# Starting the first feed-forward group on half of its tokens, packed apart, in a fused linear-attention and maxout kernel

## The chip, the cores and the metric

One NeuronCore of a Trainium2 chip runs the whole program. The metric is the device time of one execution in microseconds (us). Times are medians of several runs; a ratio is the mean time of one kernel's fast runs over the mean of the other's fast runs of the same rounds, so it is not quite the ratio of the medians quoted. The span of a profile is 1.7 to 1.9 us (once 2.0) shorter than the time of the same run.

## The reference

```python
# q, k, v, f_logit: (4 batches, 8 heads, 768 tokens, 48); fp32
f = 1 / (1 + exp(-f_logit))
for t in range(768):                       # per batch and head
    state = f[t][:, None] * state + outer(k[t], v[t])
    y[t] = q[t] @ state
x = y.transpose(0, 2, 1, 3).reshape(3072, 384)
h = maximum(maximum(x @ w1, x @ w2), x @ w3)        # 384 x 768 each
out = h @ w_out                                     # 768 x 384
```

The kernel cuts the sequence into 24 units of 128 tokens (64 of each of two batches). Four units make a group of 512 tokens, the width of one feed-forward (FFN) matmul.

## The kernel before

Each unit's attention part is split into stages that the program interleaves by hand: `sigmoids`, `after` (scan of the gates from behind, then kh), `before` (scan from the front, then qh), `keys` (transposes), `pairs`, `values`, `finish`. The FFN of a group is a generator, and `fill(n)` runs n of its steps between attention stages of the next group, so that TensorE never stands.

```python
def round_begin(n):      # ScalarE, two passes over raw piece n
def round_middle(n):     # VectorE max and shift (L224, L225), GpSimd add (L227)
def round_end(n):        # VectorE merge into w_in or w_out (L234)

def pack(u0, u1, xT, queues=one):      # heads -> xT: TEN DMAs, whatever the number of tokens
    ...
def ffn(g, xT):
    for j in range(NJ):                # 6 column blocks
        for i in range(3):             # w1, w2, w3: one "step", 512 tokens wide
            ... 3 matmuls into p
            if i == 0: nc.scalar.copy(top, p)
            else:      nc.vector.tensor_tensor(hm[:, j, :] if i == 2 else top, p, top, op=ALU.max)
            if g == 0: ... round one piece, begin another, load_weights(2, r + 1)
            yield
    ... 4 output blocks (w_out), a yield behind each

def busy(n): ...                       # n dummy matmuls, 256 wide

# ... (loads and units 0 to 2)
load_weights(3); load(GRP, one, "fk")  # f and k of unit 4
pairs(3); busy(1); round_begin(2); round_middle(2)
values(3); round_end(0)
finish(3)                              # state update L359, heads of unit 3
round_end(1); round_end(2)
pack(0, GRP - 1, xT, both)             # all 512 tokens, SyncE and ScalarE
for n in range(3, 5): round_begin(n); round_middle(n)
busy(14)                               # dummies while xT is packed
load(GRP, one, "q"); load_v(GRP); load_weights(3); load(GRP + 1); load_v(GRP + 1)
pending.append(ffn(0, xT))
fill(1); sigmoids(GRP); after(GRP); fill(1); before(GRP); carry(GRP); fill(1)
# ... units 4 to 23, four fills each
fill(8)
# tail: least = min(ends); one matmul over it (L581); fill(99)
```

## Time and profile before

| | before |
|---|---|
| median (range) beside the changed kernel | 488.15 us (487.48 to 489.26, 4 runs) |
| span of the profiled run | 487.8 us (a further run, of 489.5 us) |
| TensorE busy | 466.6 us, 96% |
| end of unit 3's state update, T | 33.3 us |
| first FFN matmul | 42.1 us |
| pairs of unit 8 (start) | 112.15 us |

From unit 8 on both kernels do nearly the same work in nearly the same order, so the start of the pairs of unit 8 is a good milestone. The lines of the profile are in the prediction.

### The profile page before, as it was taken

The numbers are of one execution on the slowest core, as the hardware profiler recorded it, in microseconds if no ns is written. First come the engines' busy times: TensorE is split into PE (matmuls) and PEld (weight loads), VectorE is DVE, ScalarE is ACT, GpSimd is POOL, SyncE is SP. The second block draws the span as 40 slices with busy tenths as digits, with TensorE's granted clock in tenths as the row PEclk, the third lists the DMA queues.
The fourth block names the chain that finished last, engine by engine and source line by source line (L and its number), as shares of the span: only waits on it lengthen the run. The fifth ranks groups of instructions, "written<-read, shape, count | busy, mean of one in ns | idle before, by whom it ended". The sixth has DMA issues, their size and how long they took to land.

```text
span 487.8 us, 10037 instructions
## 1 busy us (share of the span) xinstructions
PE 466.6 (96%) x4101; PEld 252.5 (52%) x4101; DVE 223.2 (46%) x346; ACT 109.4 (22%) x227; POOL 99.5 (20%) x132
## 2 busy tenths in 40 slices
PE   5779999998999999999999999999999999989994
PEld 4666465555454446555546554556554445434452
DVE  7954999993263462263462253462354320112110
ACT  2344445333022112122112122122121112000000
POOL 2122456553120220211220211220211300000000
PEclk9979999999999999999999999999999999999998
DMA  9987999633664042565042674033630012100012
GB/s 128 161 201 202 257 233 198 92 76 66 110 87 66 1 79 47 101 83 84 1 79 53 106 91 66 0 67 65 107 43 1 1 48 50 32 1 1 0 23 48
DMA packets 170008, 38.51 MB, mean 79 GB/s; under 512 B 154977, under 2 KB 168801, under 8 KB 169953
## 3 DMA queue, kind: packets, MB, share of 16 engines
q1 hardware_dynamic: 166208, 36.50, 42.6%
q10 hardware_dynamic: 3744, 1.28, 1.3%
q8 instruction: 34, 0.56, 0.5%
q14 instruction: 22, 0.17, 0.1%
HBM read 28.31 MB, written 4.72 MB: 68 GB/s over the span
## 4 chain that ended last, share of the span: by engine, by line
PE 87%; SPq 5%; DMA 3%; DVE 1%; ACT 1%; issue 1%; POOL 0%; ACTq 0%; DVEq 0%; POOLq 0%
PE p L401 55%; PE p L422 19%; SPq L159 3%; PE y L342 3%; PE y L372 2%; PE a L328 2%; PE y L351 2%; PE p L448 2%; PE tr L315 1%; SPq L174 1%; DMA raw<-in_moe_w_dram 1%; PE tr L243 1%; DMA k_ld<-in_k_dram 1%; SPq L389 1%; DMA v_ld<-in_v_dram 1%
## 5 line engine op out<-in xcount | busy, mean ns | idle before, releaser
L401 PE MATMUL p<-xT,w_in 128*128 128x512 f32 x648 | 288.1, 596 | 0.7 <-ACT top L405 0.7
L401 PEld LDWEIGHTS p<-xT,w_in 128*128 128x128 f32 x648 | 120.0, 190 | 138.4 <-issue 132.0
L422 PE MATMUL p<-w_out,hm 128*128 128x384 f32 x288 | 96.6, 490 | 0.5 <-DVE w_out L234 0.5
L407 DVE TENSOR_TENSOR top<-p,top 128x512 f32<-128x512 f32 x36 | 24.7, 687 | 119.1 <-PE p L401 118.9
L422 PEld LDWEIGHTS p<-w_out,hm 128*128 128x128 f32 x288 | 53.8, 190 | 38.1 <-issue 2.4
L405 ACT COPY top<-p 128x512 f32<-128x512 f32 x36 | 21.1, 586 | 179.2 <-PE p L401 179.2
L407 DVE TENSOR_TENSOR hm<-p,top 128x512 f32<-128x512 f32 x36 | 24.8, 690 | 50.5 <-PE p L401 50.5
L288 POOL COPY ends<-r 128x8 f32<-128x8 f32 x24 | 4.7, 194 | 189.3 <-DVE r L282 189.3
L227 POOL TENSOR_TENSOR top_bits<-top_bits,rest_bits 128x384 uint32<-128x384 uint32 x24 | 28.3, 1178 | 40.2 <-DVE top_bits L225 25.5
L427 ACT COPY o<-p 128x384 f32<-128x384 f32 x24 | 11.5, 477 | 106.8 <-PE p L422 103.6
L296 DVE TENSOR_TENSOR_SCAN prod<-gate,from_inv 128x520 f32<-128x520 f32 x24 | 34.7, 1448 | 0.0
L282 DVE TENSOR_TENSOR_SCAN r<-gate,from_one 128x520 f32<-128x520 f32 x24 | 30.9, 1289 | 2.8 <-issue 2.1
L378 ACT COPY heads<-y 64x256 f32<-64x256 f32 (+1 forms) x72 | 26.6, 369 | 9.5 <-PE y L372 8.3
L331 DVE TENSOR_TENSOR at<-a,mask 128x512 f32<-128x512 f32 x24 | 16.5, 688 | 24.9 <-PE a L328 24.9
L300 POOL TENSOR_TENSOR qh<-qt,prod 128x512 f32<-128x512 f32 x16 | 18.8, 1178 | 38.1 <-DVE qt L247 38.1
L342 PEld LDWEIGHTS y<-at,v_ld 64*64 64x64 f32 x768 | 14.4, 137 | 18.1 <-issue 15.0
L289 POOL TENSOR_TENSOR kh<-kt,r 128x512 f32<-128x512 f32 x16 | 19.7, 1233 | 14.0 <-DVE kt L247 14.0
L317 ACT COPY ks<-tr 128x512 f32<-128x512 f32 x22 | 12.9, 585 | 39.3 <-PE tr L315 39.0
L306 POOL TENSOR_TENSOR state<-st,ends 128x384 f32<-128x384 f32 x22 | 20.4, 925 | 0.2
L342 PE MATMUL y<-at,v_ld 64*64 64x64 f32 x768 | 18.0, 228 | 2.5 <-ACT heads L378 1.4
L247 DVE STREAM_TRANSPOSE gate<-sig 128x512 f32<-128x512 f32 x16 | 11.3, 708 | 16.8 <-ACT sig L263 16.8
L224 DVE TENSOR_SCALAR top_bits<-top_bits 128x384 f32<-128x384 f32 x24 | 12.6, 525 | 9.9 <-ACT top_bits L212 9.9
(66 smaller groups left out, 286.5 us busy)
## 6 DMA issues: line engine op xcount, KB each, us to landing
raw<-in_moe_w_dram SPq DMA_DIRECT2D x18, 384.0 KB, 6.0
v_ld<-in_v_dram SPq DMA_DIRECT2D x48, 96.0 KB, 3.1
out_dram<-o SPq DMA_DIRECT2D x48, 96.0 KB, 2.2
raw<-in_moe_w_out_dram SPq DMA_DIRECT2D x6, 384.0 KB, 5.8
xT<-heads SPq DMA_DIRECT2D x30, 72.0 KB, 2.2
f_ld<-in_f_logit_dram SPq DMA_DIRECT2D x32, 64.0 KB, 2.6
k_ld<-in_k_dram SPq DMA_DIRECT2D x32, 64.0 KB, 2.6
q_ld<-in_q_dram SPq DMA_DIRECT2D x32, 64.0 KB, 2.5
```

Source lines behind the costliest of these rows:

```text
L227: nc.gpsimd.tensor_tensor(top, top, rest, op=ALU.add)
L282: nc.vector.tensor_tensor_scan(r[:, 0:LEN][:, ::-1], flat(gate)[:, ::-1], flat(from_one)[:, ::-1], 1.0, op0=ALU.mult, op1=ALU.max)
L289: (nc.vector if u < BY_ROWS else nc.gpsimd).tensor_tensor(kh.rearrange("p h a t -> p a h t"), kt, by_batch(r[:, 1:LEN + 1].rearrange("p (x ...
L296: nc.vector.tensor_tensor_scan(flat(prod), flat(gate_tiles[u % 2]), flat(from_inv[u % 2]), 1.0, op0=ALU.mult, op1=ALU.max)
L300: (nc.vector if u < BY_ROWS else nc.gpsimd).tensor_tensor(qh, qt, by_batch(prod[:, :, 1:]), op=ALU.mult)
L306: nc.gpsimd.tensor_tensor(t, states[u % 2], ends[:, u, :].unsqueeze(2).to_broadcast([128, 2 * HP, D]), op=ALU.mult)
L342: nc.tensor.matmul(y[o:o + DP, a, hp * C:(hp + 1) * C], lhsT=v_ld[s, 2 * hp + par, :], rhs=d["at"][s, par, hp, :], start=(hp == 0), stop=F ...
L378: nc.scalar.copy(heads[o, :, t0 + a * C:t0 + (a + 1) * C], y[i, a, 0:HP * C].rearrange("p (h t) -> p h t", h=HP))
L401: nc.tensor.matmul(p, lhsT=w_in[i][:, kt, j * 128:(j + 1) * 128], rhs=xT[:, kt, :], start=(kt == 0), stop=(kt == NK - 1))
L405: nc.scalar.copy(top, p)
L407: nc.vector.tensor_tensor(hm[:, j, :] if i == 2 else top, p, top, op=ALU.max)
L422: nc.tensor.matmul(p[:, 0:DM], lhsT=hm[:, j, i * UT:(i + 1) * UT], rhs=w_out[:, j, :], start=(j == 0), stop=(j == NJ - 1))
```

## The change

The intent: TensorE passes some 8 us before the first FFN matmul with dummies. Pack the first 256 tokens (units 0 and 1) as soon as they are there, begin the group on them in half-wide steps, and do the other half when units 2 and 3 are packed. To make room, rounding moves behind the first units, and loads go out from two queues. Not in the cut diff: the scan is split from `after`, the stages of units 0 to 3 are reordered, the first two state copies go from VectorE to ScalarE, and xT of the first group is laid out by halves. The core of the diff, with cuts and with comments of mine:

```diff
-                load_v(0)
-                load(2)
-                load(3, one, "f")
-                load_v(1)
...
+                load_v(0, act)                 # ScalarE's queue
+                load(2, act, "k")
+                load_weights(3)                # weights ahead of f of unit 3 and v of unit 1
+                load(3, one, "f")
...
+                load_v(1, act)
...
+                pack(0, 1, xT, one, 0)         # ten DMAs more
+                load_weights(3)
+                load(GRP, one, "fk")
...
-                pack(0, GRP - 1, xT, both)
-                busy(14)
+                pack(2, 3, xT, (nc.sync, nc.scalar, nc.sync, nc.scalar, nc.sync), 1)
+                round_begin(3)
...
+            J_HALF = 2
+                steps = [(j, slice(0, TOK)) for j in range(NJ)]
+                if g == 0:    # 12 half steps, then 12 full ones
+                    steps = [(j, slice(n * HALF, (n + 1) * HALF)) for n in range(2) for j in range(J_HALF)] + steps[J_HALF:]
...
+                            ahead = n_step + 2 if n_step <= 6 else 8 + (2 * n_step - 11) // 3 if n_step <= 12 else n_step
...
-                    fill(1)
+                    fill(1 if u < 2 * GRP else 2)        # a full step now takes two fills
...
-                fill(8)
+                fill(12)
                 least = ...
+                fill(6)                                  # three steps behind the reduction
```

## The prediction

> **What bounds the kernel now.** I read the page first, then TensorE's waits after the first feed-forward (FFN) matmul, then busy time by stretch, then the timeline around the start of the FFN. Busy time of the page, and TensorE's waits from 42 us on:
>
> ```profile
> PE 466.6 (96%) x4101; PEld 252.5 (52%) x4101; DVE 223.2 (46%) x346; ACT 109.4 (22%) x227; POOL 99.5 (20%) x132
> ...
> PE a L328 <- POOL qh L300: 1.4, 1, 1.4
> PE tr L581 <- DVE least L579: 1.3, 1, 1.3
> PE p L401 <- ACT top L405: 0.7, 1, 0.7
> PE p L422 <- DVE w_out L234: 0.5, 1, 0.5
> ```
>
> Once the FFN has begun, TensorE waits 1.4 + 1.3 + 0.7 + 0.5 = 3.9 us in all. So the span is 42.1 (start of the first FFN matmul) + 435.3 (work) + 3.9 (waits) + 6.5 (last output copy and stores, 481.3 to 487.8) = 487.8. Only the start and the waits can change.
>
> Busy time by stretch; columns: us from:to, length, then busy us and count of PE, PEld, DVE, ACT, POOL, then granted clock, DMA share, GB/s:
>
> ```profile
> 10.00:12.00 2.00, 2.00 (x43) 1.61 (x41) 1.97 (x4) 0.89 (x2) 0.19 (x1) 1.00 1.53 151
> 31.00:32.00 1.00, 1.00 (x51) 1.00 (x44) 0.72 (x2) 0.42 (x1) 0.10 (x1) 0.50 0.93 207
> 33.30:42.10 8.80, 8.74 (x61) 7.43 (x62) 3.76 (x9) 3.02 (x7) 1.31 (x2) 0.76 0.53 113
> 42.10:45.90 3.80, 3.80 (x16) 2.13 (x15) 0.23 (x1) 1.05 (x3) 1.09 (x1) 1.00 0.77 164
> 45.90:108.50 62.60, 62.05 (x647) 33.70 (x646) 59.96 (x102) 28.34 (x60) 35.50 (x39) 1.00 0.88 181
> ```
>
> Until 33 us run the attention parts of units 0 to 3. From 45.9 to 108.5 both TensorE (99%) and VectorE (60.0 of 62.6, 96%) are full: VectorE rounds 24 weight pieces beside the first FFN group. Between 33.3 and 45.9 VectorE works only 4.0 us of 12.6. The timeline says why; columns: start, us, engine, line, operation, [idle before <- releaser]:
>
> ```profile
> 32.75 0.56 DVE L359 TENSOR_TENSOR st<-y,state 128x384 f32<-128x384 f32 x1 [0.99 <-PE y L351]
> 34.39 7.84 PE L448 MATMUL p<-from_one,ident 128*128 128x256 f32 x28
> 35.70 3.19 ACTq L389 DMA_DIRECT2D xT<-heads  x5
> 39.53 0.36 DVE L224 TENSOR_SCALAR top_bits<-top_bits 128x384 f32<-128x384 f32 x1 [4.82 <-ACT top_bits L212]
> 42.08 2.74 PE L401 MATMUL p<-xT,w_in 128*128 128x512 f32 x6
> 45.92 0.36 DVE L224 TENSOR_SCALAR top_bits<-top_bits 128x384 f32<-128x384 f32 x1 [3.58 <-ACT top_bits L212]
> ```
>
> TensorE fills 34.4 to 42.2 with dummy matmuls (L448) while xT is packed by DMA. VectorE waits 4.8 us for ScalarE, which is issuing five packing DMAs, and then 3.6 us for ScalarE again, which waits for the first full 512-wide FFN product.
>
> **What the Trainium skill says.** (1) "TensorE: Matmul & The Clock Gate", Part 1: an idle TensorE drops to half clock and needs a busy window of some 3.4 us to come back. The trace agrees: granted 0.50 in 31:32, still 0.76 on average in 33.3:42.1. (2) The same page, "Back-to-back issue gap": the gap grows linearly with columns, plus 2.5 ns. Six 512-wide records take 2.58 us in the chain (430 ns each), so a 256-wide one costs an estimated 215 ns: halves cost TensorE nothing. (3) "DMA: Bandwidth & Descriptors", "Issuing engines are not separate DMA queues": a second issuing engine saves only issue time. Here too: from 10 to 12 us one queue alone gives DMA share 1.53 at 151 GB/s, so the 192-byte rows already saturate it, and the second queue can only reorder. (4) "SBUF — State Buffer", "Who interferes with whom": some VectorE forms and GpSimd block each other on a shared port. L224 takes 0.35 us alone and up to 1.16 us beside GpSimd, so VectorE's queue from 45.9 to 108.5 cannot be shrunk by moving work about.
>
> **The change, part by part.** I write T for the end of the state update of unit 3 (L359): 32.75 + 0.56 = 33.3 before.
>
> *T itself.* Rounding leaves ScalarE's and VectorE's queues ahead of unit 3, and two state copies (0.56 us each) leave VectorE. That is worth about 3 us (1.4 us of TensorE behind ScalarE's copies, two roundings at about 1.1 us). Against it: ScalarE must issue four loads (v of unit 0, k of unit 2) before the sigmoid of unit 1. Each reuses one of eight DMA semaphores and waits until the load eight places earlier has landed; at 98 KB and 150 GB/s (0.655 us each) I count the fourth issued near 11.8, so that sigmoid ends at 12.4 instead of 10.3. Also three weight loads (1.2 MB, some 4 us) now precede f of unit 3, whose scan comes 1 to 1.5 us late. Walking VectorE's order with the trace's durations (scans 1.2, products 0.6 to 0.7) gives T = 32.5, a gain of only 0.8.
>
> *Start.* With the fourteen dummies gone and half A of xT packed long before, the first FFN matmul begins at T + 0.9 = 33.4 rather than 42.1: 8.7 us earlier.
>
> *What is given back at once.* The first six half steps (6 x 215 ns = 1.29 us each) need pieces 0 to 5, rounded just ahead. After T VectorE does pieces 1 and 2 in part (1.7 us), then waits for ScalarE's first pass over piece 3, which stands behind three copies of heads (1.14) and four packing DMAs (4 x 0.62 = 2.5): until about T + 5.2. Then one piece (1.1 alone, 1.4 beside GpSimd) plus a 256-wide max (0.35) per step paces TensorE: step 3 starts at T + 6.4, step 4 at 7.9, step 5 at 9.4, step 6 at 10.7 and ends at T + 12.0. Unhindered they would end at T + 0.9 + 7.7 = 8.6. So 3.4 us go back, and another 1 us around step 10, which waits for the max behind unit 4's scan. The half clock of the first two steps hides in the same wait.
>
> *The rest of the group.* VectorE's work from T to the last w_out rounding was 63.9 us (8.8 + 3.8 + 62.6 minus idle of 5.0 + 3.6 + 2.6), and 66.2 to the transposed q of unit 8 at 110.8. Now it is 66.2 + 0.65 (piece 2) + 0.24 (split maxes) = 67.1. Its idle shrinks from 11.3 to an estimated 6 (3.5 for piece 3, 1 for late raw pieces 9 to 11, 1.5 in small ones). So q of unit 8 comes at T + 73.1, and after GpSimd (1.3) the pairs of unit 8 start at T + 74.4. TensorE's own account is T + 0.9 + 68.1 (work from 42.1 to 112.15 less 2.0 waits) + 4.4 = T + 73.4. They nearly meet: VectorE decides by 1 us. With T = 32.5 that point moves from 112.15 to 106.9: 5.2 us earlier, not 8.7.
>
> *Tail.* The minimum over ends is now issued three units before the matmul that needs it, so the 1.3 us wait at L581 goes. From unit 8 on TensorE's order is unchanged.
>
> Sum: 5.2 + 1.3 = 6.5 us, 487.9 - 6.5 = 481.4; I record 481.3.
>
> **The rivals.** *A: nothing paces it.* If rounding kept up with the half steps, the whole 8.7 + 1.3 us plus most of the later waits (2.6) would come: 475 to 478. For it: the pieces are scheduled two steps ahead. Against: a half step lasts 1.29 us and a piece with its max 1.5 to 1.75 us, and VectorE is 96% full already. *B: the loads eat it.* If ScalarE's blocked loads and the weights ahead of unit 3 cost 3 us more than I count, T is 35 to 36 and the time 484 to 485. For it: DMA is saturated from 4 to 18 us. Against: the same bytes arrive before unit 3's v in both kernels. *C: the SyncE queue.* Packing now takes 16 issues on it rather than 5, and raw pieces 9 to 23 queue behind them; ScalarE would stall on raw tiles and the group end 2 to 3 us later: 483.5. The 12 pieces fetched ahead speak against.
>
> **Range and chances.** T is uncertain by 1.5 us, VectorE's idle by 2, the start by less; together about 3 us either side, with rival A's side a little longer: 477.3 to 484.8. Faster by over 2% means below 478.1, which needs rival A nearly whole: 0.14. Slower by over 2% needs a lost order of loads far beyond B: 0.01. Within 2%: 0.85.
>
> **What would show it.** Right: first FFN matmul near 33 to 34; a VectorE wait of 3 to 4 us for top_bits after the packing DMAs on ScalarE; TensorE waits of 4 to 6 us on w_in and on maxes between 33 and 60; pairs of unit 8 near 107; no wait for "least". Wrong: T under 31 or over 34.5; TensorE waiting little in the half steps (A); long waits for raw or f in the first 30 us (B) or for raw after 45 (C).

## The result, and the profile after

The changed kernel took **496.69 us** (496.54 to 496.98, 4 runs) against 488.15 us: ratio 1.0173, 95% interval 1.0153 to 1.0194. I had predicted 6.5 us less; it is 8.5 us more. The profiled run has a span of 494.8 us. (The two profiles differ by 7.0 us and not by 8.5, as that of before is of a run 1.4 us above the median.)

TensorE's waits from 30 us on in the changed kernel; columns: engine, tile, line waiting <- what it waited for: us in total, times, longest.

```profile
PE p L426 <- DVE w_in L235: 3.3, 2, 2.2
PE a L333 <- POOL qh L305: 1.9, 1, 1.9
PE p L426 <- DVE hm L433: 1.5, 1, 1.5
...
PE p L426 <- DMA xT<-heads: 0.8, 1, 0.8
PE p L426 <- DVE top L433: 0.7, 1, 0.7
```

The wait for "least" is gone, as predicted. In its place stand waits for rounded weights, for maxima, for xT and for qh. TensorE's timeline of the same stretch (start, us, engine, line, operation, count of records, [idle before <- releaser]) shows where; a half or full step is six records, `busy(n)` 2n:

```profile
36.88 1.13 PE L426 MATMUL p<-xT,w_in 128*128 128x256 f32 x4
38.84 1.97 PE L426 MATMUL p<-xT,w_in 128*128 128x256 f32 x8 [0.83 <-DMA xT<-heads]
42.98 1.78 PE L426 MATMUL p<-xT,w_in 128*128 128x256 f32 x6 [2.17 <-DVE w_in L235]
45.92 6.62 PE L426 MATMUL p<-xT,w_in 128*128 128x256 f32 x18 [1.17 <-DVE w_in L235]
...
58.60 1.56 PE L426 MATMUL p<-xT,w_in 128*128 128x256 f32 x6 [0.73 <-DVE top L433]
61.63 2.86 PE L426 MATMUL p<-xT,w_in 128*128 128x256 f32 x12 [1.47 <-DVE hm L433]
...
66.22 1.98 PE L426 MATMUL p<-xT,w_in 128*128 128x512 f32 x4
```

The first FFN matmul begins at 36.9 us, 5.2 us earlier than before. But the twelve half steps (72 records, some 15.9 us at the 0.221 us that a record takes in e10 below, and 2.9 us of unit 4's and 5's transposes and pairs among them, 18.8 in all) last until 66.2, that is 29.3 us: **10.5 us are lost inside them.** 6.4 of these are the five waits shown. About 3 are slow clock: 18 records take 6.62 us where 4.0 would do. The rest is small gaps.

SyncE's own timeline shows its queue, which issues in order; first the kernel before:

```profile
35.31 4.77 SPq L389 DMA_DIRECT2D xT<-heads  x5
40.18 1.34 SPq L159 DMA_DIRECT2D q_ld<-in_q_dram  x2
...
51.25 4.57 SPq L200 DMA_DIRECT2D raw<-in_moe_w_dram  x6
```

and the changed kernel:

```profile
28.60 7.13 SPq L399 DMA_DIRECT2D xT<-heads  x10
...
44.47 3.73 SPq L399 DMA_DIRECT2D xT<-heads  x6
48.25 1.65 SPq L201 DMA_DIRECT2D raw<-in_moe_w_dram  x3
49.99 1.37 SPq L160 DMA_DIRECT2D q_ld<-in_q_dram  x2
...
60.59 3.14 SPq L201 DMA_DIRECT2D raw<-in_moe_w_dram  x6
```

Packing by halves takes twenty DMAs instead of ten, since a DMA moves one head's piece whatever its number of tokens, and 16 of them are now on SyncE, about 0.6 to 0.7 us each. So everything behind the packing comes late: SyncE's part of the second packing, itself behind f and k of unit 4, begins at 44.5 us, q of unit 4 is issued at 50.0 instead of 40.2, and raw piece 12 at 60.6 us.

Later, at unit 8 (TensorE's timeline of the changed kernel):

```profile
118.85 0.88 PE L333 MATMUL a<-qh,kh 48*64 48x64 f32 x32 [1.94 <-POOL qh L305]
119.66 7.53 PE L452 MATMUL p<-w_out,hm 128*128 128x384 f32 x18
```

The pairs of unit 8 come at 118.85 instead of 112.15, 6.7 us later. Behind that wait the granted clock falls (0.80 from 118 to 120, 0.50 from 120 to 122 us), which costs another 1.45 us: 24 records of L452 last 9.39 us, before 7.94. So the profile adds up: -5.2 (earlier start) + 7.3 (more waiting up to unit 8) + 4.6 (slow clock and small gaps up to there) + 1.45 - 1.3 (tail) = +6.9, against +7.0 measured.

### The profile page after: what moved, and what is told of

The parts are those of the page before. It is cut to its first block, busy times and chain, and to the rows that moved or that the text cites. A ratio compares the mean times of both kernels' runs of the same rounds, so it can differ in the third digit from the quotient of the medians.

```text
span 494.8 us, 10088 instructions
## 1 busy us (share of the span) xinstructions
PE 466.6 (94%) x4111; PEld 256.9 (52%) x4111; DVE 219.8 (44%) x348; ACT 110.1 (22%) x231; POOL 101.1 (20%) x132
## 4 chain that ended last, share of the span: by engine, by line
PE 85%; DMA 5%; DVE 4%; SPq 1%; ACT 1%; issue 1%; ACTq 1%; POOL 0%; DVEq 0%; POOLq 0%
PE p L426 55%; PE p L452 19%; PE y L347 3%; PE y L377 2%; PE a L333 2%; PE y L356 2%; DMA v_ld<-in_v_dram 2%; PE tr L320 1%; DMA q_ld<-in_q_dram 1%; DMA f_ld<-in_f_logit_dram 1%; PE tr L244 1%; SPq L399 1%; DVE prod L301 1%; DMA raw<-in_moe_w_dram 1%; DVE w_in L235 1%
## 5 line engine op out<-in xcount | busy, mean ns | idle before, releaser
L426 PE MATMUL p<-xT,w_in 128*128 128x512 f32 (+1 forms) x684 | 292.4, 580 | 7.1 <-DVE w_in L235 3.3
L426 PEld LDWEIGHTS p<-xT,w_in 128*128 128x128 f32 x684 | 128.1, 192 | 142.3 <-issue 126.5
L452 PE MATMUL p<-w_out,hm 128*128 128x384 f32 x288 | 97.7, 495 | 0.0
L433 DVE TENSOR_TENSOR top<-p,top 128x512 f32<-128x512 f32 (+1 forms) x38 | 25.0, 659 | 122.3 <-PE p L426 122.1
L452 PEld LDWEIGHTS p<-w_out,hm 128*128 128x128 f32 x288 | 54.7, 193 | 38.4 <-issue 4.1
L431 ACT COPY top<-p 128x512 f32<-128x512 f32 (+1 forms) x38 | 21.4, 563 | 181.6 <-PE p L426 181.6
L433 DVE TENSOR_TENSOR hm<-p,top 128x512 f32<-128x512 f32 (+1 forms) x38 | 25.1, 662 | 52.1 <-PE p L426 52.0
L228 POOL TENSOR_TENSOR top_bits<-top_bits,rest_bits 128x384 uint32<-128x384 uint32 x24 | 28.1, 1170 | 37.7 <-DVE top_bits L226 29.3
L301 DVE TENSOR_TENSOR_SCAN prod<-gate,from_inv 128x520 f32<-128x520 f32 x24 | 35.2, 1466 | 0.0
L283 DVE TENSOR_TENSOR_SCAN r<-gate,from_one 128x520 f32<-128x520 f32 x24 | 29.7, 1239 | 6.2 <-ACT gate L261 3.3
L305 POOL TENSOR_TENSOR qh<-qt,prod 128x512 f32<-128x512 f32 x16 | 18.8, 1176 | 38.9 <-DVE qt L248 38.9
L347 PEld LDWEIGHTS y<-at,v_ld 64*64 64x64 f32 x768 | 13.6, 134 | 18.8 <-issue 15.1
L294 POOL TENSOR_TENSOR kh<-kt,r 128x512 f32<-128x512 f32 x16 | 19.7, 1234 | 13.7 <-DVE kt L248 13.0
L347 PE MATMUL y<-at,v_ld 64*64 64x64 f32 x768 | 17.0, 224 | 3.3 <-DMA v_ld<-in_v_dram 1.9
L333 PE MATMUL a<-qh,kh 48*64 48x64 f32 x768 | 16.4, 225 | 2.3 <-POOL qh L305 1.9
```

The lines of the kernel that those rows point to most:

```text
L228: nc.gpsimd.tensor_tensor(top, top, rest, op=ALU.add)
L283: nc.vector.tensor_tensor_scan(r[:, 0:LEN][:, ::-1], flat(gate)[:, ::-1], flat(from_one)[:, ::-1], 1.0, op0=ALU.mult, op1=ALU.max)
L294: (nc.vector if u < BY_ROWS else nc.gpsimd).tensor_tensor(kh.rearrange("p h a t -> p a h t"), kt, by_batch(r[:, 1:LEN + 1].rearrange("p (x ...
L301: nc.vector.tensor_tensor_scan(flat(prod), flat(gate_tiles[u % 2]), flat(from_inv[u % 2]), 1.0, op0=ALU.mult, op1=ALU.max)
L333: nc.tensor.matmul(p[t, par, hp * C:(hp + 1) * C], lhsT=kh[r, hp, a, :], rhs=qh[r, a, hp, :], start=True, stop=True)
L347: nc.tensor.matmul(y[o:o + DP, a, hp * C:(hp + 1) * C], lhsT=v_ld[s, 2 * hp + par, :], rhs=d["at"][s, par, hp, :], start=(hp == 0), stop=F ...
```

## The experiments

Eighteen kernels ran, in five batches on five chips. Each batch has its own runs of the kernel before, and there they scatter more: 486.1 to 492.5 us. That scatter goes with the granted clock of the run: in one batch 486.07 us at 0.999, 489.37 at 0.990, 490.66 at 0.985. So I read shares of 1 us or less from the traces, not from the medians. "Pairs of unit 8" is the milestone named above; ratios are against the kernel before.

| run | what | median us | ratio (95%) | T | pairs of unit 8 |
|---|---|---|---|---|---|
| e1 | after, loads of before | 495.88 | 1.014 (1.007, 1.021) | 33.6 | 117.7 |
| e2 | before, loads of after | 492.00 | 1.008 (1.001, 1.015) | 37.4 | 114.3 |
| e3 | after, piece 3 begun early | 497.03 | 1.019 (1.011, 1.026) | 35.0 | 117.5 |
| e4 | after, dummies in the waits | 497.89 | 1.019 (1.012, 1.026) | 35.9 | 119.9 |
| e5 | after, e1 + e3 + queue reordered | 495.41 | 1.016 (1.012, 1.021) | 32.7 | 116.4 |
| e6 | after, cheap rounding (wrong) | 494.44 | 1.015 (1.010, 1.019) | 36.1 | 116.2 |
| e7 | before, cheap rounding (wrong) | 487.72 | 1.001 (0.997, 1.005) | 32.0 | 108.5 |
| e8 | before, three half steps | 491.79 | 1.010 (1.005, 1.015) | 31.9 | 113.4 |
| e9 | e5, cheap rounding (wrong) | 494.86 | 1.011 (1.005, 1.016) | 35.1 | 119.9 |
| e10 | e9 with 12 dummies | 495.31 | 1.013 (1.008, 1.018) | 34.3 | 117.9 |
| e11 | before, late fill and tail moved | 486.98 | 0.995 (0.991, 0.999) | 32.6 | |
| e12 | after, late fills put back | 501.20 | 1.027 (1.022, 1.032) | 35.2 | |
| e13 | after, no loads of units 4, 5 (wrong) | 497.20 | 1.019 (1.014, 1.024) | 37.3 | 119.4 |
| e14 | e13, cheap rounding (wrong) | 487.57 | 0.997 (0.993, 1.002) | 36.7 | 110.5 |
| e15 | e14, loads of before (wrong) | 488.43 | 0.999 (0.995, 1.004) | 33.8 | 111.5 |
| e16 | after, half steps undone | 495.27 | 1.012 (1.006, 1.017) | 40.2 | 119.5 |
| e17 | e8, loads moved | 490.90 | 1.004 (1.001, 1.006) | 32.7 | 113.2 |
| e18 | e11, dummies ahead of v of unit 3 | **483.86** | 0.989 (0.987, 0.992) | 31.5 | |

(Pairs of unit 8 are left out where a block was moved across them.) T of the seven profiles that have the changed kernel's loads and half steps (the changed kernel, e3, e4, e6, e12 to e14) lies from 35.0 to 37.3, mean 36.1; of the five with half steps and the loads of before (e1, e5, e9, e10, e15) from 32.7 to 35.1, mean 33.9. So the loads move T by some 2 us, and one profile by itself can be as far off.

### First: which single part does it? (e1 to e4)

**e1** puts the order of loads of before into the changed kernel, **e2** the order of after into the kernel before:

```diff
 e1: +load_v(0); load(2); load(3, one, "f"); load_v(1); load(3, one, "kq"); load_v(2); load_weights(3); load_v(3); load_weights(3)
     -load_v(0, act); load(2, act, "k"); load_weights(3); ... load_v(1, act) ...
 e2: the reverse, in the kernel before
```

> The changed kernel with the load order and queues of the kernel before (all on SyncE's queue, the first weights behind v of unit 2); everything else of the change stays. Theory L (the new loads make the attention part late: end of unit 3's state update at 36.2 instead of 33.3): that point comes back to 32.5 to 33.5, the first FFN matmul to 33.5 to 34.5, and the time falls by about 3 us to 493.5. Rival D (VectorE's total work up to the last rounded piece decides, as I predicted): it also falls by about 3. Rival Q (raw pieces and queue decide): the time stays within 1 us of 496.7.

> The kernel before with the load order and queues of the changed one, nothing else. Theory L: end of unit 3's state update moves from 33.3 to about 36, the first FFN matmul from 42.1 to 45, the time rises by about 3 us to 491. If the loads are harmless by themselves and only the interplay hurts: 488, within 1 us.

e1 brought T back to 33.6 us, and the time hardly moved: 495.88. In place of the late start its TensorE waits 2.4 us for xT, 2.5 for q of unit 4 and 1.4 for top. e2 came out at 492.0 with T = 37.4, so the loads by themselves do harm in a kernel without half steps (though the interval of its ratio begins at 1.0005). Where the time goes is in the chain of the changed kernel (start, us, what):

```profile
14.46 8.48 DMA v_ld<-in_v_dram
22.93 0.04 issue
22.98 0.62 PE y L347 x25
```

v of unit 1, issued by ScalarE at 13.8 and 14.5 us, lands only at 22.9. In the kernel before it was issued at 14.1 and 14.8 us, no earlier, and TensorE had it at 19.7. New ahead of it are three weight loads of 384 KB, issued at 12.4 to 13.9; a second queue did not get it past them. That these three are the reason is read from the order: no run moved them alone. f of unit 3, issued at 15.2 and 15.9, took 7.8 us to land as well, and in e2 the chain runs through f and not through v:

```profile
16.10 7.94 DMA f_ld<-in_f_logit_dram
```

There TensorE waits 2.1 us for f of unit 3 and nothing for v.

**e3** begins piece 3 ahead of ScalarE's packing DMAs, **e4** puts 5 and 3 dummies into the two waits before half steps 3 and 4:

```diff
 e3:  round_begin(2)
     +round_begin(3)                     # was behind pack(2, 3, ...)
 e4: +warm = {2: 5, 3: 3}.get(n_step, 0) if g == 0 else 0
     +for _ in range(warm): nc.tensor.matmul(pw, lhsT=ident, rhs=from_one..., start=True, stop=True)
```

> The changed kernel with ScalarE's first pass over weight piece 3 moved ahead of its four packing DMAs; one call moved. Theory R (the half steps wait for rounded pieces because the first pass stands behind those DMAs): the VectorE wait of 3.8 us at 37.8 goes, half step 3 starts near 41 instead of 43.0, step 4 near 43 instead of 45.9, and the time falls by 2 to 3 us; by 5 to 6 if the closed gaps also keep the clock up (theory C on top). Rival D (VectorE's total decides): the wait only moves, the time stays within 1 us of 496.7.

> The changed kernel with five dummy matmuls in TensorE's wait before half step 3 and three before step 4, about as long as the waits (2.2 and 1.2 us). Theory C (the waits drop the granted clock to 0.50 from 44.4 to 50.9, and steps 4 to 6 take 6.6 us instead of 3.9): the clock stays at 1.00, the time falls by 2.5 to 3 us. If VectorE paces the steps anyway (theory R alone): steps 4 to 6 end no sooner, the time stays within 0.7 us of 496.7.

Neither gained. In e3 the wait for w_in shrank from 3.3 to 0.8 us, and q of unit 4 was then 2.6 us late. In e4 the clock stayed at 1.00 through the half steps, and what it saved turned into a wait of 2.9 us for q and 1.7 for top. So the slow clock, 3 of the 10.5 us lost, was no cause: it hid behind a supply that came later anyway.

### Then: which supply? (e5 to e7, e9, e10)

**e5** is e1 and e3 with SyncE's queue reordered (all loads of unit 4 right behind the packing, pieces 12 and 13 ahead of unit 5). **e6** and **e7** cut the rounding of each piece to its last VectorE operation, in the changed kernel and in the one before:

```diff
 e5: +load(GRP)                          # f, k, q right behind pack(2, 3, ...)
     +load_weights(2, 2); pending.append(ffn(0, xT)); fill(2); load(GRP + 1); load_v(GRP + 1); fill(4)
 e6, e7: round_begin, round_middle: -all
         round_end: -by(top)  +by(hi)
```

> The changed kernel with the loads of before (as e1), piece 3 begun early (as e3), and SyncE's queue reordered behind the packing: f, k and q of unit 4 directly behind the second packing, weight pieces 12 and 13 ahead of unit 5's loads, and those two half steps later. Theory S (after the packing the in-order queue delivers q of unit 4 and pieces from 12 on too late; in e1 and e3 TensorE waited 2.5 us for q and VectorE 3.5 us for piece 12 at 60 to 64): both waits shrink to under 1 us, and the time falls by 3 to 5 us to 492 or 493. If VectorE's and GpSimd's rounding itself is the pace in that stretch (theory R): the waits go but the time stays within 1.5 us of e1 (495.9).

> The changed kernel with the rounding of each weight piece cut to one VectorE operation (wrong values on purpose: no ScalarE passes, no GpSimd addition, one VectorE operation instead of three). Theory R (rounded pieces pace the half steps): with no rounding to wait for, the waits on w_in and maxes go, the clock stays up, the first FFN matmul comes at 34 to 36 and the time falls by 10 us or more, to 483 to 486, below the cheap kernel of before. Theory S (loads and queue): waits for q of unit 4 and for raw pieces take their place, the time stays above 490.

> The same cut of the rounding in the kernel before. It never waited for rounded pieces except 0.5 us, and its start is set by the packing: both theories expect only what ScalarE's freed queue gives at the start, 1 to 2 us, so 486 to 487.

e5 (495.41) no longer waits more than 0.7 us for a load of unit 4, but 2.4 us for top, 1.5 for hm, 2.1 for xT. e6 (494.44) has no wait for rounding, but one line stands out in TensorE's timeline:

```profile
55.53 1.09 PE L229 MATMUL tr<-ident,q_ld 128*128 128x128 f32 x4 [4.62 <-DMA q_ld<-in_q_dram]
```

q of unit 4, again issued at 49.3 us, landed 5.3 us later behind three raw pieces. I had expected e6 to tell whether rounding was the bound; it told that rounding is not the only one. e7 shows that rounding doesn't bound the kernel before: 487.72, its ratio 1.001.

**e9** joins e5 and e6, **e10** adds `busy(12)` before the first half step:

> The reordered queue of e5 together with the one-operation rounding of e6 (wrong values on purpose). Each alone left the time at 494 to 495; in e5 the TensorE waits were the rounding's (top 2.4, hm 1.5 us), in e6 the load's (q of unit 4, 4.6 us). Theory S+R (two supplies, the rounding and the queue of loads, bound the early stage side by side, so that removing one uncovers the other): the waits for top, hm and q of unit 4 all vanish, full steps begin by about 60 us instead of 63.9 to 64.2, and the time falls by some 3.9 to 4.6 us to about 491. Rival L (the stage near 112 to 119 us, with the chain to qh of unit 8, is a fixed date): full steps begin earlier but the pairs of unit 8 stay near 116 us and the time stays 494 to 495.

> e9 with 12 dummy matmuls ahead of the first half step, so that it begins with all of xT there and at full clock. In e5 the first 36 matmuls lasted from 33.7 to 46.9 us: three waits for xT of 2.1 us in sum and half the clock from 36 to 42 us. Theory S+R with a third term, cold start (the clock): dummies end at about 36.1, the 36 matmuls take 36 x 0.22 = 7.9 us and end at 44.0, some 2.9 us earlier than in e9, and the time falls by as much, to about 488. If the clock hides behind other waits, as in e4, the time is that of e9 within 1 us.

Both missed: 494.86 and 495.31. The waits for top, hm and q went as expected, and pairs of unit 4 came at 60.0 and 59.1 us; but then TensorE waited 4.0 and 3.9 us for f of *unit 5*, which my order had put behind raw pieces 12 and 13. I had moved the shortage, not removed it. To take it away the loads themselves had to go.

### The deciding pair (e13, e14), and e15

**e13** is the changed kernel without the 16 loads of units 4 and 5; their tiles keep the tokens of units 0 and 1. Its output is wrong, which doesn't matter for the time. **e14** adds the cheap rounding of e6. **e15** adds to that the loads of before and piece 3 begun early.

```diff
 def load_tokens(dst, src, u, queues=one):
+    if u in (GRP, GRP + 1):
+        return
```

> The changed kernel without the 16 loads of units 4 and 5 (f, k, q and v; the tiles keep the tokens of units 0 and 1, wrong values on purpose). SyncE, which issues in order and spent 0.65 to 0.85 us on each DMA between 28 and 60 us, gets some 10 us back. Theory Q (SyncE's issuing, made longer by ten more packing DMAs, is what ate the gain): the raw piece 12, issued at 60.6 us, comes by about 50, the wait for hm at 61.6 and those for q of unit 4 cannot arise, full steps begin 2 to 4 us earlier than 66.2, time 493 to 494.5. Theory R (the rounding, alone, once the loads are no bound): time as of the changed kernel within 1 us.

> The same with the one-operation rounding (wrong twice on purpose). In e6, with the cheap rounding alone, the only large wait was 4.6 us for q of unit 4. Theory Q+R (two supplies bound it together): that wait goes and no other takes its place, full steps begin near 59 us instead of 64.2, pairs of unit 8 near 111 instead of 116.2, time about 489. If something else is the bound (rival X, unknown), the pairs of unit 8 stay near 116 and the time near 494.

> The same with the load order of before and piece 3 begun early, so that the state update ends at 33.6 us again instead of 36.2. Theory Q+R with the third term of the sum, the late v of unit 1: another 2 to 3 us, less what the wait for xT takes back (2 us in e1 and e5) and the cold clock behind it: first half step at 34 us, time 487 to 488.5, so the earlier start is worth having only when nothing else has to be supplied. If the time is that of e14 within 1 us, xT took it back in full.

| changed kernel | loads of units 4, 5 kept | taken away |
|---|---|---|
| rounding kept | 496.69 | 497.20 (e13) |
| rounding cheap | 494.44 (e6) | **487.57** (e14) |

(The three experiments and the changed kernel ran in different batches; by ratio to before the four are 1.017, 1.019, 1.015 and 0.997.) Neither alone gives more than some 2 us; both together give 9. This is the picture of two supplies that end at about the same time. One control is missing: the kernel before without those loads was not run. It can hardly have 9 us to gain there, since from its first FFN matmul on TensorE waits 3.9 us in all, and for no load. Busy time from 42 to 62 us (columns as in the prediction: PE, PEld, DVE, ACT, POOL, clock, DMA share, GB/s) shows the same, for the changed kernel and, below it, for e13:

```profile
42.00:62.00 20.00, 15.65 (x62) 12.13 (x63) 18.50 (x35) 9.28 (x22) 11.40 (x10) 0.83 0.90 156
42.00:62.00 20.00, 12.98 (x60) 9.92 (x60) 19.04 (x33) 10.82 (x25) 11.39 (x10) 1.00 0.77 249
```

and for e14:

```profile
42.00:62.00 20.00, 19.88 (x124) 15.84 (x125) 14.55 (x27) 3.49 (x7) 2.34 (x5) 1.00 0.87 295
```

and, for comparison, the kernel before:

```profile
42.00:62.00 20.00, 20.00 (x158) 10.66 (x156) 15.56 (x28) 9.54 (x19) 9.06 (x9) 1.00 1.12 257
```

In e13 VectorE is busy 19.0 of 20 us and TensorE 13.0: TensorE waits 5.2 us for w_in, 2.0 for top, 1.5 for hm. In e14 TensorE is busy 19.9 (a wait of 1.8 us for ScalarE's copy of top, behind its packing DMAs, ends at 42.0). The kernel before has TensorE full *and* VectorE at 15.6: a full step gives VectorE 2.6 us per weight piece. A half step uses up a piece in half that time. **Beginning on half of the tokens doubles the rate at which weights must be ready** in half steps 1 to 6, which take pieces 0 to 5, and in this kernel the weights come from VectorE. Half steps 7 to 12 use the same six pieces again; there VectorE rounds ahead for the full steps, and the waits of steps 10 and 11 are for maxima that stand in its queue behind this rounding and the scans of unit 4. VectorE's timeline of the changed kernel shows how far off that rate was:

```profile
41.61 0.36 DVE L225 TENSOR_SCALAR top_bits<-top_bits 128x384 f32<-128x384 f32 x1 [3.78 <-ACT top_bits L213]
42.00 0.36 DVE L226 TENSOR_SCALAR top_bits<-top_bits 128x384 uint32<-128x384 uint32 x1
42.28 0.55 DVE L235 SCALAR_TENSOR_TENSOR w_in<-raw,top_bits 128x384 uint32<-128x384 uint32 x1
42.76 1.16 DVE L225 TENSOR_SCALAR top_bits<-top_bits 128x384 f32<-128x384 f32 x1
...
44.56 1.31 DVE L235 SCALAR_TENSOR_TENSOR w_in<-raw,top_bits 128x384 uint32<-128x384 uint32 x1
```

An operation that takes 0.35 or 0.55 us alone takes 1.16 or 1.31 beside GpSimd's addition (42.51 to 43.70, 44.46 to 45.45), which belongs to another piece. From one L235 to the next pass 2.3 and 2.2 us (42.28, 44.56, 46.78), a max in each, not the 1.5 of my prediction; TensorE could have used a piece every 1.3 us.

e15 shows what remained of the early start when nothing was short: T came back to 33.8, 2.9 us earlier than e14's, and the pairs of unit 8 were not earlier (111.5 against 110.5): TensorE stood 0.5 us for xT and 0.8 us for nothing that the trace names, and 32 half-wide records took 10.2 us where 7.1 would do. So even with weights and tokens for nothing the change only drew level (0.997 and 0.999), while the kernel before with cheap rounding has its pairs of unit 8 at 108.5. The chips and clocks of those profiles differ, so of this last comparison I keep only that no gain of 5 us is in sight.

What the pair does not separate: taking the loads away frees SyncE's issuing (some 0.65 us for each of 16) and the DMA traffic behind it (1.5 MB, in e6 at a DMA share of 1.41 from 52 to 56 us). Which of the two made q late is not settled. In the changed kernel itself TensorE does not wait for q; that wait shows once something else comes sooner (e1, e3, e4, e6).

### How much is the half part's? (e16, e8, e17)

**e16** undoes the half part alone: one packing of ten DMAs, no half steps, `busy(14)`, the rounding pace of before; loads, new order of scans and tail stay.

```diff
-            J_HALF = 2
+            J_HALF = 0
...
-                pack(0, 1, xT, one, 0)
...
-                pack(2, 3, xT, (nc.sync, nc.scalar, nc.sync, nc.scalar, nc.sync), 1)
+                pack(0, GRP - 1, xT, both)
...
+                busy(14)
```

> The changed kernel with the half part alone undone: one packing of ten DMAs on two queues, no half steps, 14 dummies and the rounding pace of before; the loads on two queues, the pulled apart scan and the tail stay. Account so far: loads alone cost the kernel before 3.8 us (e2, 492.0), the tail gives 1.3 back. Theory Q+R: the rest of the loss, some 4 us, is the half part's, so this lies at 490.7 to 492.5. Rival (the half part is harmless and the loads and the new order of scans and fills make the loss): 495 to 497.

495.27 us, in runs from 492.4 to 497.3: nearer to the rival than to the theory, which had given the half part some 4 us. The profiled run is one of the slowest; TensorE there stood 2.0 us inside the values of unit 3 with no wait that the trace shows, and T came at 40.2. So the shares cannot be added: loads alone cost 0.8% (e2), everything but the half part 1.2% (e16), everything but the loads 1.4% (e1), all of it 1.7%. Nor is it the same loss: in e16's profile the first FFN matmul comes at 49.4 us, 7.3 us later than before, and the pairs of unit 8 7.4 later, so everything is lost ahead of the FFN, while the changed kernel begins the FFN 5.2 us early and loses in the half steps. How much of e16's late T is its stop, how much the loads (e2: 37.4) and how much the new order of scans and copies was not tested.

**e8** is the gentlest form I found: loads, order and pace of the kernel before, with three half steps of the first column block in place of most dummies, and the tail moved. **e17** is e8 with f of unit 4 loaded by ScalarE and k right behind the packing.

```diff
 e8:  +pack(0, 1, xT, one, 0)            # early, units 0 and 1
      -pack(0, GRP - 1, xT, both); busy(14)
      +pack(2, 3, xT, both, 1); busy(5); J_HALF = 1
 e17: +load(GRP, act, "f")               # ahead of round_begin(3)
      +load(GRP, one, "k"); load_weights(3); load(GRP, one, "q")   # behind the packing
```

> An attempt at a version that beats both: loads, rounding and packing of before, but units 0 and 1 packed early and apart, and only three half steps (the first output block, pieces 0 to 2, which before has rounded by then) put in the place of most of the 14 dummy matmuls; piece 3 begun early; the check of the minimum moved as in the change. Theory R: nothing unrounded is needed early, so TensorE saves 3 half steps (3.9 us) and the 1.3 us wait at the end, less what VectorE can't follow: 483 to 485. If starting on halves is a loss by itself: 488 or more.

> e8 with the loads it lacked: e8 (half steps of the first column block alone, in place of most dummies, with the loads and the rounding pace of before) lost 4.5 us waiting for k of unit 4, which SyncE issued only at 42.6 us, behind 15 packing DMAs and three raw pieces. Here f of unit 4 goes to ScalarE ahead of piece 3, and k is the first load behind the packing (about 39.5 us). Theory Q (SyncE's in-order issuing is the bound there): the wait for k falls under 1 us, the profile by some 4 us under e8's 487.6, and the time by some 3 to 4 us to 488 (e8 491.8), that is level with before. Rival: the next thing late (raw pieces 4 to 6, which ScalarE already waited for in e8 at 44.7 us, or q) takes it back and the time stays near 491.

e8 took 491.79 and waited 4.5 us for k of unit 4; e17 took 490.90. Its wait for k was gone, but SyncE needed from 29.5 to 41.7 us for its 15 packing DMAs, xT was waited for 3.1 us and q 1.5. By the medians the rival of e17 is right; by the ratios (1.004 against e8's 1.010, with overlapping intervals) e17 may have gained up to some 0.6% on e8, but its interval begins at 1.001, so it is not level with before. With these ten DMAs on the queue I found no order in which all that is needed by 45 us is there.

### The late stage and a better kernel (e11, e12, e18)

**e12** puts two output blocks back between values of unit 7 and keys of unit 8, where the change had left none. **e11** does the like with one block in the kernel before, and moves the reduction of `ends` forward as the change did:

```diff
 e12: -fill(1 if u < 2 * GRP else 2)
      +fill(4 if u == 2 * GRP - 1 else 1 if u < 2 * GRP else 2)
 e11: -fill(1)                            # unit 7
      +fill(2 if u == 2 * GRP - 1 else 1)
      -fill(8)
      +fill(6)
       least = ...
      +fill(3)
```

> The changed kernel with two output blocks put back between values of unit 7 and keys of unit 8, where the rebuilt counts of fill left none: there TensorE waits 0.6 and 1.9 us, and the clock then falls to 0.50 for some 3 us and costs 1.4 us. Theory L (part of the loss is made here, not in the early stage): waits and clock dip go, the time falls by 2.5 to 3.9 us to about 493. Theory E (early stage alone; the 2.5 us are a wait for VectorE that comes out the same at the next unit): time as of the changed kernel within 1 us.

> The kernel before with two small moves only: one more block of the first group's output matmuls between values of unit 7 and keys of unit 8, where TensorE waits 0.55 and 1.42 us, and the reduction of ends six steps into the last group instead of eight with three steps behind it, as in the changed kernel, where that wait of 1.3 us vanished. Theory: both waits go, the profile gains 1.4 to 2.0 plus 1.3 us: 484.5 to 485.3, ratio 0.993 to 0.995. Rival: the pairs of unit 8 are decided by VectorE's total work, and what is put in front only moves the wait to unit 9: gain 1.3 us alone, ratio 0.997.

e12 was wrong: 501.20. The waits at unit 8 and the slow clock went, but the blocks taken from behind unit 8 had covered the packing of the second group:

```profile
PE p L426 <- DMA xT<-heads: 6.5, 1, 6.5
```

So the gap at unit 8 was no free loss. e11 gave 486.98, ratio 0.995: the 1.3 us of the tail came, and of the 2.0 us at unit 8 nearly all was lost again at unit 9 (a stop of 1.7 us in L401 with no releaser in the trace).

Eight profiles have a stop of this kind, of 0.2 to 2.8 us; in five of them (e1, e9, e10, e15, e16) it stands behind the same 13th record of unit 3's state product, in e2 behind the 15th, in e11 and e18 at unit 9. The DMA view, asked by quarters of a microsecond, shows one packet of the kind "instruction" (0.02 MB) ahead of each, and TensorE goes on 2.2 to 3.4 us after it, whether the stop is short or long (e10: packet at 30.5, stop from 32.7 to 33.1; e9: 31.0, 31.1 to 33.9; e11: 124.5, 125.6 to 127.3; e18: 120.8, 121.8 to 123.2). This points to the fetching of TensorE's instructions. No run tests it, other such packets pass without a stop, and shorter stops in the first half step of e9 and e15 do not fit. If it is so, e11's loss at unit 9 is no wait for VectorE, as its rival has it.

**e18** adds to e11 three dummy matmuls ("pairs", since each is two records) ahead of the values of unit 3. TensorE waits there, 1.4 us in before (by its trace for ScalarE's copy of heads, not for v) and 1.8 us for v in e11:

```diff
 pairs(3)
-busy(1)
+busy(4)
```

> e11 and three more dummy pairs ahead of values of unit 3 in the kernel before. There TensorE waits 1.4 us for v (before) or 1.6 to 1.8 us (e11), after which the clock falls to 0.56 to 0.73 and the 28 dummies last 7.8 (before) and 9.0 us (e11) instead of 6.3 (e7, at full clock, first full step at 38.75 us). Theory K (the kernel before loses up to 3 us to that cold start, which also makes its scatter of 486 to 492 us from run to run): the clock stays at 1.00, the first full step begins near 39 to 40.5 us, and the time is 484 to 486, ratio 0.985 to 0.992. Rival: what is begun earlier waits later for rounding or loads, as in the changed kernel: ratio 0.995 as e11.

It took **483.86 us** (483.06 to 484.53, 6 runs), ratio 0.9894 (0.9869 to 0.9920), correct, and beats both kernels: 5.2 us below the median of before in its batch. TensorE's timeline:

```profile
27.72 1.99 PE L448 MATMUL p<-from_one,ident 128*128 128x256 f32 x8
...
32.15 6.31 PE L448 MATMUL p<-from_one,ident 128*128 128x256 f32 x28
38.29 2.74 PE L401 MATMUL p<-xT,w_in 128*128 128x512 f32 x6
```

The 28 records of the dummies last 6.3 us instead of 7.8: the granted clock, 0.50 from 32 to 36 us in before, is 1.00 from 26 to 38 us here. The first FFN matmul comes at 38.3 instead of 42.1 us, 3.8 us earlier, at full width and with SyncE's queue as it was. The scatter shrank from 4.6 us to 1.5. (T was 31.5 here, 1.8 earlier than in the profile of before; part of that is chance, as e7 had T near 32 as well. Against e11, whose profile is of its slowest run, T is 1.1 earlier and the dummies take 6.3 instead of 9.0 us, so the first FFN matmul comes 4.2 us earlier and the time of the profiled run is 4.0 less.)

## Why the prediction was wrong, step by step

Two steps failed: the size of T, and that VectorE alone paces the stretch up to unit 8. One term, the cost of a piece per half step, was mis-sized. In order:

- **T itself** (predicted 32.5, measured 36.2). This step failed. I set the gain on ScalarE and VectorE against the loads and saw the three weight loads delay f of unit 3 by 1 to 1.5 us. In the run v of unit 1, which I had left out, landed 8.5 us after its issue, some 3 us later than before, and TensorE waits 1.9 us for it; f of unit 3 took 7.8 us to land. The argument against rival B, "the same bytes arrive before unit 3's v in both kernels", looked at the wrong unit: the state of unit 1 is needed for unit 3's. B's T of 35 to 36 so came near; its time of 484 to 485 did not, and the late T is not what the loss hangs on: e1 takes it away and gains less than 1 us by the median (0.4% by the ratio).
- **Start at T + 0.9** (measured 36.24 + 0.64). Right. But half A of xT was not "packed long before": SyncE issued its ten DMAs from 28.6 to 35.7, and TensorE waits 0.8 us for it within the first step.
- **Step 3 at T + 6.4** (measured T + 6.7), behind a VectorE wait of 3.8 us for ScalarE's packing DMAs. Right in mechanism and size.
- **Step 4 at T + 7.9, end of step 6 at T + 12.0** (measured T + 9.7 and T + 16.2). This is the term that was mis-sized: I counted 1.4 us for a piece beside GpSimd, and a max; the trace has 2.2 us from piece to piece with the max, as one operation of each is held up by 0.8 us. The 1.16 us that I had quoted from the trace of before already said so. "The half clock hides in the same wait" held for the first steps; from 44 to 51 us the clock was low again, yet e4 shows that this cost no time by itself.
- **Another 1 us around step 10.** In truth 0.7 and 1.5 us at steps 10 and 11. Together, 10.5 us are lost in the twelve half steps, where I gave back 4.4.
- **VectorE decides the pairs of unit 8, T + 74.4** (measured T + 82.6). Failed: with rounding almost free (e6) the time fell by only 2 us. Rival C, the SyncE queue, to which I gave 2 to 3 us because twelve pieces were fetched ahead, bound the start beside VectorE (e13 and e14). Its sign came true as well: ScalarE stands 3.9 us for raw piece 12, until 64.5. And I had looked at raw pieces and not at q, k and f of units 4 and 5, which stand in the same queue. My three rivals were weighed one at a time; here C stood beside the rounding, and each hid the other.
- **Tail, 1.3 us.** Right, in the changed kernel and in e11.
- **From unit 8 on TensorE's order is unchanged.** Nearly; but the rebuilt counts of fill left no block ahead of unit 8, and the slow clock behind that wait cost 1.45 us.

The 14% that I gave to "faster by over 2%" and the range down to 477 rested on rounding alone being the pace.

## What to carry to other kernels

An earlier start is worth only what can be fed to it: count for every engine and every in-order queue what the early steps need and when it comes. The first steps of half width use up new weights twice as fast for the same TensorE time, and a packing by halves costs as many DMAs again. When a change makes several supplies tight at once, taking one away may show nothing; take away pairs before calling one of them innocent. And look first at what the dummies and the clock do: three more dummy matmuls in the right place, with two small moves, gave 5 us where the rebuild lost 8.

## What the Trainium skill lacked or had wrong

- "DMA: Bandwidth & Descriptors", "Issuing engines are not separate DMA queues" calls the sequencer time to initiate a DMA "usually small relative to the DMA itself". Here it was 0.6 to 0.7 us for each DMA, of 8 to 96 KB, one after the other: ten packing DMAs held SyncE for 7.1 us, fifteen for 12.2 us (e17, with its waits in it), while a single one of them lands after some 2 us. The section's other statement, that a second issuing engine gives no lane of its own, agrees with the runs: v of unit 1, issued by ScalarE behind weights issued by SyncE, took 8.5 us to land.
- "TensorE: Matmul & The Clock Gate", Part 1, has the clock fall after about 3.4 us of idleness. In the kernel before a single wait of 1.4 us, with TensorE busy 1.0 of the 2 us from 28 to 30, was followed by 0.50 from 32 to 36 us; in the changed kernel waits of 0.6 and 1.9 us within 5 us were. With dummies in the wait (e18) it stayed up. But 1.4 us at unit 8 of the kernel before and 1.7 us in e11 had no fall behind them (1.00 from 110 to 118 and from 124 to 132 us). So idleness well under a whole window can be enough, and need not be; what decides, the runs don't say.
- "SBUF — State Buffer", "Who interferes with whom", says that the loser of the shared port is blocked for the whole instruction. The runs agree (0.35 to 1.16 us, 0.55 to 1.31 us), so nothing is wrong there. Here one of the three VectorE operations of a rounding meets GpSimd's addition for another piece, so a piece and its max take 2.2 us, where the piece's three operations alone take 1.26.
